# 47-point DFT of later batches as three float32r products, with the inputs taken through a DRAM buffer

## The chip, the core and the metric

The kernel runs on one core of one Trainium2 chip. The time is the device time of one execution in microseconds (us); several executions are timed, and their median is given. The engines are TensorE (PE in the profile, with its weight loads as PEld), VectorE (DVE), ScalarE (ACT), GpSimd (POOL) and SyncE (SP, which here issues nearly all DMAs after the first batch).

## The reference

A convolution along the sequence by a real FFT, and then, for each token, a two-layer network with a rational function between the layers:

```python
X = np.fft.rfft(x, axis=1)                  # x: 8 batches, 3008 positions, 256 channels
y = np.fft.irfft(X * (filt_r + 1j * filt_i), n=3008, axis=1)
h = y.reshape(24064, 256) @ w_in            # 256 x 2048
P = a[0] + a[1] * h + a[2] * h**2 + a[3] * h**3
Q = 1.0 + abs(b[0]) * abs(h) + abs(b[1]) * h**2
out = (P / (Q + 1e-06)) @ w_out             # 2048 x 256
```

## The kernel before

3008 = 64 x 47, so the Fourier transform is split in stages of matrix products. Stage 1 is the 47-point DFT: the input of a batch, laid out beforehand as 96 rows (47 positions and one of padding, times two halves) by 32 x 256 columns (`xp`), is multiplied by a constant 96 x 96 matrix. A batch has eight loads q of 96 x 1024 numbers (tile `xin`, 384 KB each, 4 KB in a row), and each load two products of 96 x 512 (tile `s`, matmul on L298). ACT evicts each product from PSUM into `ev` (`s1e` in the profile), and SP stores the pair into a DRAM buffer `scr1`. Stage 2 loads `scr1` in another layout, multiplies by the 64-point matrix (`y`, L346), by the filter (DVE and POOL), and by the inverse matrix (`z`, L379), and stores into `scr2`. Stage 3 loads `scr2` (tile `tl`), does the inverse 47-point product (`x`, L424), and writes the result as two float32r tiles, `xh` and the remainder `xl`, which feed the network.

Stages 1 to 3 multiply float32 by float32. The network multiplies in float32r: each operand is split into a float32r part and a float32r remainder, and three products hi x hi, lo x hi and hi x lo are summed in PSUM.

The network's work is cut into 752 units: unit i is 512 tokens by 128 of the 2048 hidden columns, 16 units to a token tile. A unit has six float32r products into `h_u` (L457, L458, L460), five activations on ACT, four operations on DVE (L502, `hi_u` on L511, L519, `lo_u` on L525), two on POOL (L497, then L516, the product q * hi), and six float32r products into `o` (L534 to L536). The operations of a unit are spread over several steps: at step i TensorE does the `h_u` products of unit i and the `o` products of unit i-4, and the other engines work on units i to i-3, by a list of lags.

`pipeline` writes this out by hand: for the engines PE, ACT, DVE and POOL the order in the code is the order of execution. At every step at most one piece of the next batch's convolution is put behind the unit's `h_u` products. Pieces are paid from a credit that grows by 0.6 a unit while batch 1 is prepared, and by 0.38 for later batches; the number that a generator yields is a piece's price, and a bare `yield` hands on to the next place in the step, or the next step, without a price. SP's order is not written by hand once the pipeline has begun: a list scheduler puts SP's DMAs where it finds them ready. Every DMA of SP takes one of eight semaphores in turn, and waits for the DMA that had it before.

Batch 0 goes through all stages before the units begin, together with the decoding of the weights' 64-bit words (`bits` and `split`), of which the last four of 16 steps run beside the first units. Batches 1 to 7 are prepared beside the units. The code branches once, on a flag from the scalars, into one of two versions of the pipeline.

Of the kernel before, what the change touches and what calls it, by code (L numbers as in the profile page):

```python
# [9 lines left out]
F32 = mybir.dt.float32  # L10
F32R = mybir.dt.float32r
I32 = mybir.dt.int32
U32 = mybir.dt.uint32
AF = mybir.ActivationFunctionType
ALU = mybir.AluOpType
# [9 lines left out]
NH = 32  # L25
K2 = 24
R1 = 96
C = 256
# [6 lines left out]
XF = 1  # L35
RING = dict(a=4, w=3, q=5, hi=5, lo=4)
GAP = 4
PGAP, XGAP = 1, 1
CPOS = 3
OG = 2  # L40
# [2 lines left out]
EV1, EV2, EVO = "A", "AV", "AV"  # L43
XB, FB = 4, 3
# [12 lines left out]
TT = 512  # L57
# [45 lines left out]
def conv_moe(ctx: ExitStack, tc: tile.TileContext, xp, fr, fi, w_in, w_out, ab, mats, small, sgn, outT):  # L103
    nc = tc.nc
    B = xp.shape[0]

    consts = ctx.enter_context(tc.tile_pool(name="consts", bufs=1))
    dram = ctx.enter_context(tc.tile_pool(name="dram", bufs=3, space=DRAM))
    conv = ctx.enter_context(tc.tile_pool(name="conv", bufs=2))
# [9 lines left out]
    xh = xl = None  # L119
    mats_sb = consts.tile([128, 3, 128], F32, name="mats_sb")  # L120
    small_sb = consts.tile([R1, R1 + GE], F32, name="small_sb")
    a1_sb, e_sb = small_sb[:, :R1], small_sb[:, R1 : R1 + G]
    words = consts.tile([128, 128], F32, name="words_sb")
    sgn_sb, ab_sb, abs_sb, cf_sb = words[:, :K2], words[:, 32:44], words[:, 64:76], words[:, 96:120]
    flag_sb = words[:, 120:121].bitcast(I32)
# [28 lines left out]
    def inverse(y, x, t):  # L154
        v.reciprocal(y, x)
        tt(out=t, in0=x, in1=y, op=ALU.mult)
        ts(out=t, in0=t, scalar1=-1.0, scalar2=2.0, op0=ALU.mult, op1=ALU.add)
        tt(out=y, in0=y, in1=t, op=ALU.mult)

    def square_scalars():  # L160


        x, y, z, p, ip, pq1 = (col(i, 2) for i in (8, 10, 12, 14, 16, 18))
        v.tensor_copy(col(8), A3)
        v.tensor_copy(col(9), B1)
        inverse(y, x, z)

        stt(out=col(14), in0=A2, scalar=0.5, in1=col(10), op0=ALU.mult, op1=ALU.mult)
        stt(out=col(15), in0=B0, scalar=0.5, in1=col(11), op0=ALU.mult, op1=ALU.mult)
        inverse(ip, p, z)  # L170
        v.tensor_copy(IPC, col(16))
        v.tensor_copy(IQC, col(17))
        tt(out=ip, in0=ip, in1=ip, op=ALU.mult)
        tt(out=pq1[:, :1], in0=A1, in1=col(10), op=ALU.mult)
        ts(out=pq1[:, 1:], in0=col(11), scalar1=1.000001, scalar2=None, op0=ALU.mult)
        tt(out=pq1, in0=pq1, in1=ip, op=ALU.mult)
        ts(out=pq1, in0=pq1, scalar1=1.0, scalar2=None, op0=ALU.subtract)
        v.tensor_copy(PK, col(18))
        stt(out=P0, in0=A0, scalar=col(10), in1=col(16), op0=ALU.mult, op1=ALU.mult)
        inverse(IK, col(19), col(12))  # L180
        ts(out=SGN, in0=IK, scalar1=0.0, scalar2=None, op0=ALU.is_ge)
        ts(out=SGN, in0=SGN, scalar1=2.0, scalar2=-1.0, op0=ALU.mult, op1=ALU.add)
        tt(out=AIK, in0=IK, in1=SGN, op=ALU.mult)

        inverse(col(20), col(16), col(12))
        stt(out=col(20), in0=A3, scalar=col(20), in1=AIK, op0=ALU.mult, op1=ALU.mult)
        stt(out=SC, in0=col(11), scalar=col(17), in1=col(20), op0=ALU.mult, op1=ALU.mult)
        for name, c in (("ipc", IPC), ("iqc", IQC), ("ik", IK), ("sc", SC)):
            act_scale[name] = r = nc.scalar.alloc_register(name)
            nc.scalar.reg_load(r, c[:1].bitcast(I32))  # L190
# [4 lines left out]
    class Weights:  # L195
# [14 lines left out]
        def load(self):  # L210
            tag = ("oe", "tl", "oe", "tl", "raw")[self.i % 5] if self.i < HD else ("oe", "xin")[self.i % 2]
            raw = conv.tile([128, 2 * TT], I32, tag=tag, name=f"raw{self.i}", bufs={"xin": XB, "raw": 1}.get(tag))
            self.raw = raw.rearrange("p (n t) -> p n t", t=2)
            (nc.scalar if self.i < HD else nc.sync).dma_start(raw.rearrange("p (a c) -> p a c", a=2), self.src)
# [38 lines left out]
        return wo_sb[:, f // 2, k, c : c + 128]  # L253

    scr1 = [dram.tile([K2, 128, C], F32, tag="scr1", name=f"scr1_{b}") for b in range(B)]
    scr2 = [dram.tile([K2, 128, C], F32, tag="scr2", name=f"scr2_{b}") for b in range(B)]

    def rows(scr):
        return scr.rearrange("k (g m) c -> (k g) m c", m=NH)

    def evac(which, out, in_, i):
        if which[i % len(which)] == "A":
            nc.scalar.activation(out, in_, AF.Copy)
        else:
            nc.vector.tensor_copy(out, in_)
# [17 lines left out]
    def stage1_load(b, q):  # L283
        xin = conv.tile([R1, 2, TT], F32, tag="xin", name=f"xin{b}_{q}", bufs=XB)
        nc.sync.dma_start(
            xin.rearrange("p a b -> p (a b)"), xp[b, :, 4 * q : 4 * q + 4, :].rearrange("p m c -> p (m c)")
        )
        return xin

    def stage1(b, q, xin=None):  # L290

        if xin is None:
            xin = stage1_load(b, q)
        ev = conv.tile([R1, 2, TT], F32, tag="ev", name=f"s1e{b}_{q}")
        for j in range(2):
            yield 0.86
            k, pt = banks.tile(f"s1_{b}_{q}_{j}")
            nc.tensor.matmul(pt[:R1], a1_sb, xin[:, j], start=True, stop=True)  # L298
            yield
            evac(EV1, ev[:, j], pt[:R1], 2 * q + j)  # L300
            banks.done(k, 0.5)
        nc.sync.dma_start(
            rows(scr1[b])[:, 4 * q : 4 * q + 4, :].rearrange("r m c -> r (m c)"), ev.rearrange("p a b -> p (a b)")
        )

    class Stage2:

# [81 lines left out]
    def stage2(b):  # L389
        s = Stage2(b)  # L390
        for q in range(2):
            s.load_filter(q)
            s.load(q)
        for i in range(13):
            if i < 12:
                yield from s.product(i)
            if i > 0:
                yield from s.inverse(i - 1)
            if i % 2 == 0 and i // 2 + 2 < 6:
                s.load_filter(i // 2 + 2)  # L400
                s.load(i // 2 + 2)
            if i > 0 and i % 2 == 0:
                s.store(i // 2 - 1)
# [134 lines left out]
    banks = None  # L538
# [12 lines left out]
    nt = B * S // T  # L551

    def conv_items(b):
        for q in range(8):
            yield from stage1(b, q)
        for _ in range(GAP):
            yield
        yield from stage2(b)

    def run(gen):  # L560
        for _ in gen:
            pass
# [3 lines left out]
    class Decode:  # L566
# [19 lines left out]
        def part(self, k):  # L586
            while self.parted < k:
                weights[self.parted].split()
                self.parted += 1
# [3 lines left out]
    def first_batch():  # L593

        s = Stage2(0)
        s.more = [xpool.tile([128, 6 - FB, 4, C], F32, tag=x, name=f"f{x}") for x in ("xh", "xl")]
        xin = {}
        fl = iter(range(6))

        def do(tokens):  # L600
            for c in tokens:
                if c == "W":
                    dec.load()
                elif c == "D":
                    dec.step()
                elif c == "F":
                    s.load_filter(next(fl))

        nc.scalar.dma_start(ab_sb, ab.rearrange("(o n) -> o n", o=1).broadcast_to([128, 12]))
        nc.scalar.dma_start(small_sb, small)  # L610
        for q in range(XB):
            xin[q] = stage1_load(0, q)
        do("WW")
        nc.scalar.dma_start(mats_sb, mats)
        nc.scalar.dma_start(sgn_sb, sgn)
        load_flag()
        square_scalars()
        for q in range(8):
            run(stage1(0, q, xin.pop(q)))
            if q + XB < 8:  # L620
                xin[q + XB] = stage1_load(0, q + XB)
            do(HA[q])
        for q in range(XB - 1):
            s.load(q)
        for q in range(2):
            s.double_filter(q)
        do(HM)
        for i in range(12 + ZL):
            if i < 12:
                run(s.product(i))  # L630
            if i >= ZL:
                run(s.inverse(i - ZL))
            q, j = divmod(i, 2)
            if j == 0 and q + XB - 1 < 6:
                s.load(q + XB - 1)
            elif j and q + 2 < 6:
                s.double_filter(q + 2)
            if i > ZL and (i - ZL) % 2:
                s.store((i - ZL) // 2)
            do(HB[i])  # L640
        nonlocal xh, xl
        xh, xl = (xpool.tile([128, 2, RX], F32R, tag=x, name=x) for x in ("xh", "xl"))
        for k in range(2):
            run(stage3(k))
        dec.part(HD)
        assert dec.done == dec.loaded == HD
# [99 lines left out]
    with tc.manual_schedule(engines=ENGINES):  # L746
        banks = Banks(8 - T * 2 // TT)
# [70 lines left out]
```

## Time and profile before

| | |
|---|---|
| median of 3 runs | 2541.02 us (2540.35 to 2542.63) |
| profiled execution | 2545.82 us, of which the span of instructions 2543.2 us |
| mean granted TensorE clock | 0.991 |
| stage-1 products | 128, of which 112 for batches 1 to 7 |
| DMA traffic | 208.76 MB, mean 82 GB/s |

In the profile a line begins with the line number in the code, then engine, operation, output and input. Busy time is the time in which an engine had at least one instruction under way. On TensorE matmuls are pipelined, so an instruction's length is more than the distance to the next one, and distances between starts are what counts. The rows of windows give, for a stretch in us, the busy time and the number of instructions of PE, PEld, DVE, ACT and POOL, then the granted clock, the share of the 16 DMA engines' time that was busy, and GB/s. A float32 matmul has two records.

### The profile page before, as it was taken

How to read it: one execution, taken by the hardware profiler on the slowest of the kernel's cores; microseconds unless marked ns; L12 is line 12 of the kernel's file. 1: busy time of each engine (PE TensorE's matmuls, PEld its weight loads, DVE VectorE, ACT ScalarE, POOL GpSimd, SP SyncE). 2: the span in 40 equal slices, each digit the busy share in tenths (PEclk: the TensorE clock that was granted, in tenths of full speed). 3: DMA queues.
4: the chain of work that ended last, by engine and by line, in shares of the span. 5: the costliest groups of instructions: out<-in, count | busy, mean ns of one | idle time of the engine just before them, and what ended most of it. 6: DMA issues, size and time to landing. Idle time of an engine off the chain costs nothing.

```text
span 2543.2 us, 35887 instructions
## 1 busy us (share of the span) xinstructions
PE 2479.4 (97%) x10712; PEld 1934.2 (76%) x10712; DVE 2264.1 (89%) x3549; ACT 2197.0 (86%) x4170; POOL 1850.8 (73%) x1984
## 2 busy tenths in 40 slices
PE   4799999999999999999999999999999999999998
PEld 1467777777777777777777777777777778888887
DVE  4789988999889998899888998899988999999998
ACT  3588889888998889888998889988888889999997
POOL 2468876788668876788667886688767887677676
PEclk7899999999999999999999999999999999999999
DMA  8653341323223332233213332233322210000000
GB/s 239 192 138 114 97 120 48 113 84 98 68 81 93 91 87 64 79 98 96 83 56 106 93 96 70 72 93 99 89 62 89 72 55 28 25 25 17 25 9 19
DMA packets 102813, 208.76 MB, mean 82 GB/s; under 512 B 8752, under 2 KB 58512, under 8 KB 102608
## 3 DMA queue, kind: packets, MB, share of 16 engines
q1 hardware_dynamic: 99568, 199.79, 26.8%
q10 hardware_dynamic: 3040, 6.58, 0.9%
q8 instruction: 87, 1.43, 0.2%
q14 instruction: 118, 0.97, 0.1%
HBM read 131.36 MB, written 74.97 MB: 81 GB/s over the span
## 4 chain that ended last, share of the span: by engine, by line
PE 93%; DVE 2%; DMA 2%; ACT 1%; issue 0%; SPq 0%; ACTq 0%; DVEq 0%
PE o L534 13%; PE o L535 13%; PE o L536 13%; PE h_u L458 13%; PE h_u L457 13%; PE h_u L460 13%; PE x L424 4%; PE s L298 4%; PE y L346 3%; PE z L379 3%; DMA scr<-s1e 1%; DMA fxl<-fi 0%; DVE hi_u L511 0%; DVE h_u L519 0%; ACT q_u L478 0%
## 5 line engine op out<-in xcount | busy, mean ns | idle before, releaser
L516 POOL TENSOR_TENSOR q_u<-q_u,hi_u 128x512 f32<-128x512 f32 x752 | 973.7, 1295 | 493.4 <-DVE hi_u L511 475.7
L534 PE MATMUL o<-hi_u,wo_sb 128*128 128x512 f32 x1504 | 701.0, 466 | 0.0
L465 ACT ACTIVATE q_u<-h_u 128x512 f32<-128x512 f32 x752 | 449.9, 598 | 203.8 <-PE h_u L460 150.8
L511 DVE SCALAR_TENSOR_TENSOR hi_u<-h_u,words_sb,a_u 128x512 fp32r<-128x512 f32 x752 | 561.7, 747 | 60.3 <-ACT a_u L487 57.6
L519 DVE SCALAR_TENSOR_TENSOR h_u<-h_u,words_sb,q_u 128x512 f32<-128x512 f32 x752 | 567.1, 754 | 52.4 <-POOL q_u L516 52.1
L457 PE MATMUL h_u<-xh,wi_sb 128*128 128x512 f32 x1504 | 596.3, 396 | 5.4 <-DVE xl L435 4.0
L535 PE MATMUL o<-lo_u,wo_sb 128*128 128x512 f32 x1504 | 589.6, 392 | 1.6 <-DVE lo_u L525 1.6
L536 PE MATMUL o<-hi_u,wo_sb 128*128 128x512 f32 x1504 | 589.3, 392 | 0.0
L458 PE MATMUL h_u<-xl,wi_sb 128*128 128x512 f32 x1504 | 588.2, 391 | 0.0
L497 POOL TENSOR_SCALAR q_u<-q_u,words_sb 128x512 f32<-128x512 f32 x752 | 579.3, 770 | 3.5 <-ACT a_u L482 3.5
L502 DVE SCALAR_TENSOR_TENSOR h_u<-w_u,words_sb,h_u 128x512 f32<-128x512 f32 x752 | 563.3, 749 | 4.2 <-ACT w_u L472 4.2
L525 DVE TENSOR_TENSOR lo_u<-h_u,a_u 128x512 fp32r<-128x512 f32 x752 | 516.4, 687 | 0.1
L482 ACT ACTIVATE a_u<-q_u 128x512 f32<-128x512 f32 x752 | 475.4, 632 | 0.1
L487 ACT ACTIVATE a_u<-a_u 128x512 f32<-128x512 f32 x752 | 470.4, 626 | 0.0
L478 ACT ACTIVATE q_u<-q_u 128x512 f32<-128x512 f32 x752 | 469.5, 624 | 0.0
L460 PE MATMUL h_u<-xh,wi_sb 128*128 128x512 f32 x1504 | 464.6, 390 | 0.0
L472 ACT ACTIVATE w_u<-h_u 128x512 f32<-128x512 f32 x752 | 443.8, 590 | 0.0
L534 PEld LDWEIGHTS o<-hi_u,wo_sb 128*128 128x128 f32 x1504 | 283.2, 188 | 112.2 <-issue 63.3
L535 PEld LDWEIGHTS o<-lo_u,wo_sb 128*128 128x128 f32 x1504 | 283.2, 188 | 111.3 <-issue 60.0
L457 PEld LDWEIGHTS h_u<-xh,wi_sb 128*128 128x128 f32 x1504 | 283.0, 188 | 73.6 <-DVE lo_u L525 4.3
L458 PEld LDWEIGHTS h_u<-xl,wi_sb 128*128 128x128 f32 x1504 | 283.3, 188 | 64.5 <-issue 4.1
L536 PEld LDWEIGHTS o<-hi_u,wo_sb 128*128 128x128 f32 x1504 | 282.5, 188 | 61.8
(96 smaller groups left out, 1886.7 us busy)
## 6 DMA issues: line engine op xcount, KB each, us to landing
xin<-xp SPq DMA_DIRECT2D x64, 384.0 KB, 3.9
scr<-s1e SPq DMA_DIRECT2D x64, 384.0 KB, 4.1
xin<-scr SPq DMA_DIRECT2D x48, 512.0 KB, 4.9
scr<-ev SPq DMA_DIRECT2D x48, 512.0 KB, 4.7
outT<-oe SPq DMA_DIRECT2D x47, 512.0 KB, 3.3
f<-fr SPq DMA_DIRECT2D x87, 256.0 KB, 4.1
f<-fi SPq DMA_DIRECT2D x87, 256.0 KB, 3.8
tl<-scr SPq DMA_DIRECT2D x44, 480.0 KB, 4.0
```

Source lines behind the costliest of these rows:

```text
L457: nc.tensor.matmul(o, w_in_part(0, f, cc), xh[:, cc, ts], start=cc == 0, stop=False)
L458: nc.tensor.matmul(o, w_in_part(0, f, cc), xl[:, cc, ts], start=False, stop=False)
L460: nc.tensor.matmul(o, w_in_part(1, f, cc), xh[:, cc, ts], start=False, stop=cc == 1)
L497: nc.gpsimd.tensor_scalar(out=self.q, in0=self.q, scalar1=AIK, scalar2=SGN, op0=ALU.mult, op1=ALU.add)
L502: v.scalar_tensor_tensor(out=H, in0=w, scalar=PK, in1=H, op0=ALU.add, op1=ALU.mult)
L511: nc.vector.scalar_tensor_tensor(out=self.hi, in0=self.H, scalar=self.p0, in1=self.a, op0=ALU.add, op1=ALU.mult)
L516: nc.gpsimd.tensor_tensor(out=self.q, in0=self.q, in1=self.hi.bitcast(F32), op=ALU.mult)
L519: nc.vector.scalar_tensor_tensor(out=self.H, in0=self.H, scalar=self.p0, in1=self.q, op0=ALU.add, op1=ALU.subtract)
L525: nc.vector.tensor_tensor(out=self.lo, in0=self.H, in1=self.a, op=ALU.mult)
L534: nc.tensor.matmul(o, w_out_part(0, f, dd), self.hi, start=f == 0, stop=False)
L535: nc.tensor.matmul(o, w_out_part(0, f, dd), self.lo, start=False, stop=False)
L536: nc.tensor.matmul(o, w_out_part(1, f, dd), self.hi, start=False, stop=f == 15)
```

## The change

For batches 1 to 7 stage 1 is done by `stage1_parts` instead of `stage1`. SP first copies each load's 384 KB from `xp` into a DRAM buffer `scr0`, and loads `xin` from there, as a float32r tile. For each half of a load (a "part") ACT copies `xin` into a float32r tile `xh` (one of the tag `raw`, with a single buffer), POOL subtracts it from `xin` in place, and TensorE does three float32r products in place of one float32 product, with the constant matrix split in the same way once at the start (`a1r_sb`). The price of a product goes from 0.86 to 0.69. The part of product i+1 is put between the products and the eviction of product i; before the first product there are three bare yields. The eviction on ACT, the store and the stages behind it stay.

```diff
+    a1r_sb = consts.tile([R1, 2, R1], F32R, name="a1r_sb")
+    scr0 = [None] + [dram.tile([R1, NH, C], F32, tag="scr0", name=f"scr0_{b}", bufs=2) for b in range(1, B)]
+    def stage1_parts(b):
+        xin, his = {}, {}
+        def copy(q):
+            m = slice(4 * q, 4 * q + 4)
+            nc.sync.dma_start(scr0[b][:, m], xp[b, :, m])
+        def load(q):
+            xin[q] = conv.tile([R1, 2, TT], F32R, tag="xin", name=f"xin{b}_{q}", bufs=XB)
+            src = scr0[b][:, 4 * q : 4 * q + 4].rearrange("p m c -> p (m c)")
+            nc.sync.dma_start(xin[q].bitcast(F32).rearrange("p a b -> p (a b)"), src)
+        def part(i):
+            q, j = divmod(i, 2)
+            if j == 0:
+                his[q] = conv.tile([R1, 2, TT], F32R, tag="raw", name=f"xh{b}_{q}", bufs=1)
+            x, hi = xin[q][:, j], his[q][:, j]
+            nc.scalar.activation(hi, x.bitcast(F32), AF.Copy)
+            nc.gpsimd.tensor_tensor(out=x, in0=x.bitcast(F32), in1=hi.bitcast(F32), op=ALU.subtract)
+        for q in range(3):
+            copy(q)
+        load(0)
+        load(1)
+        yield 0.1
+        for _ in range(PART):          # PART = 3
+            yield
+        part(0)
+        for i in range(16):
+            q, j = divmod(i, 2)
+            if j == 0:
+                ev = conv.tile([R1, 2, TT], F32, tag="ev", name=f"s1e{b}_{q}")
+                if q + 3 < 8:
+                    copy(q + 3)
+                if q + 2 < 8:
+                    load(q + 2)
+            yield 0.69
+            k, pt = banks.tile(f"s1_{b}_{q}_{j}")
+            hi, lo = his[q][:, j], xin[q][:, j]
+            nc.tensor.matmul(pt[:R1], a1r_sb[:, 0], hi, start=True, stop=False)
+            nc.tensor.matmul(pt[:R1], a1r_sb[:, 0], lo, start=False, stop=False)
+            nc.tensor.matmul(pt[:R1], a1r_sb[:, 1], hi, start=False, stop=True)
+            yield
+            if i < 15:
+                part(i + 1)
+            evac(EV1, ev[:, j], pt[:R1], i)
...
     def conv_items(b):
-        for q in range(8):
-            yield from stage1(b, q)
+        yield from stage1_parts(b)
...
+        nc.scalar.activation(a1r_sb[:, 0], a1_sb, AF.Copy)
+        nc.gpsimd.tensor_tensor(out=a1r_sb[:, 1], in0=a1_sb, in1=a1r_sb[:, 0].bitcast(F32), op=ALU.subtract)
```

How the queues change. In the lists below a line number is that of the version it is from; the first digit in a name like `xin1_3` is the batch and the second the load, `scr0_4` is the copy buffer of batch 4, `raw15` a piece of the weights, `tl3` a chunk of stage 3, `f11_0` and `f21_0` the filter's two tables for batch 1, and `x5` means that many alike in a row.

SP, from the first entries behind the branch. Before:

```order
L214 DMA raw14_645<-w_out 128x2x512
L418 DMA tl2_668<-scr2_0_88 96x1280
L285 DMA xin1_0_670<-xp 96x1024
L214 DMA raw15_723<-w_out 128x2x512
L285 DMA xin1_1_806<-xp 96x1024
L418 DMA tl3_976<-scr2_0_88 96x1280
L285 DMA xin1_2_889<-xp 96x1024
L418 DMA tl4_1256<-scr2_0_88 96x1280
L285 DMA xin1_3_957<-xp 96x1024
```

SP at the same place, changed (shown without a break up to the fourth load of batch 1):

```order
L320 DMA xin1_1_685<-scr0_1_89 96x1024
L216 DMA raw15_726<-w_out 128x2x512
L315 DMA scr0_2_90<-xp 96x1024 x6
L315 DMA scr0_3_91<-xp 96x1024 x2
L320 DMA xin1_2_759<-scr0_1_89 96x1024
L315 DMA scr0_3_91<-xp 96x1024 x6
L315 DMA scr0_4_92<-xp 96x1024 x8
L315 DMA scr0_5_93<-xp 96x1024
L379 DMA f11_0_1746<-fr 64x1024 x2
L315 DMA scr0_5_93<-xp 96x1024 x5
L474 DMA tl4_1304<-scr2_0_96 96x1280
L379 DMA f21_0_1747<-fi 64x1024
```

The copies of batches 2 to 5 stand ahead of batch 1's fourth load `xin1_3`, which is the next row; ten copies and `tl3` stand ahead of these rows, and the rest of the 56 copies stand between `xin1_3` and the seventh load, `xin1_6`, so that none is left behind that. Between `tl2` and `xin1_6` there are 56 copies, six loads of batch 1, two stores of its products, `tl3` to `tl5`, `raw15` and twelve filter halves of 256 KB.

ACT, in two steps of batch 1 with a product (`a_u` and `q_u` are tiles of units, `s1_1_2_0` and `s1_1_2_1` are the products of load 2). Before:

```order
L465 ACTIVATE q_u7_920<-h_u7_901 128x512
L263 ACTIVATE s1e1_2_891<-s1_1_2_0_908 96x512
L487 ACTIVATE a_u6_883<-a_u6_883 128x512
L478 ACTIVATE q_u7_920<-q_u7_920 128x512
L472 ACTIVATE w_u7_921<-h_u7_901 128x512
L482 ACTIVATE a_u7_919<-q_u7_920 128x512
L465 ACTIVATE q_u8_952<-h_u8_933 128x512
L263 ACTIVATE s1e1_2_891<-s1_1_2_1_940 96x512
```

ACT in the step of product `s1_1_2_1`, changed:

```order
L538 ACTIVATE a_u12_1125<-q_u12_1126 128x512
L521 ACTIVATE q_u13_1162<-h_u13_1141 128x512
L328 ACTIVATE xh1_3_1165<-xin1_3_940 96x512
L266 ACTIVATE s1e1_2_1018<-s1_1_2_1_1148 96x512
L543 ACTIVATE a_u12_1125<-a_u12_1125 128x512
L534 ACTIVATE q_u13_1162<-q_u13_1162 128x512
```

The new Copy (L328), which needs the load `xin1_3`, stands ahead of the eviction and of the unit's further activations. The product also moved from unit 8 to unit 13.

POOL there, changed (before, the rows L553 and L572, then L497 and L516, simply alternated):

```order
L553 TENSOR_SCALAR q_u11_1091<-q_u11_1091,words_sb_80 128x512
L329 TENSOR_TENSOR xin1_3_940<-xin1_3_940,xh1_3_1165 96x512
L572 TENSOR_TENSOR q_u11_1091<-q_u11_1091,hi_u11_1158 128x512
L553 TENSOR_SCALAR q_u12_1126<-q_u12_1126,words_sb_80 128x512
L329 TENSOR_TENSOR xin1_3_940<-xin1_3_940,xh1_3_1165 96x512
```

The subtraction (L329) now stands ahead of the multiplication with `hi_u`. On TensorE one row of L298 becomes three, L350 to L352, at the same place in its step, behind the unit's `h_u` products.

More of the change, by code (lines that the diff above doesn't have):

```diff
@@ L37 @@
 GAP = 4
+PART = 3
 PGAP, XGAP = 1, 1
@@ L304, in stage1 @@
         )
+    def stage1_parts(b):
[40 more added lines that the diff above has]
+            evac(EV1, ev[:, j], pt[:R1], i)
+            banks.done(k, 0.5)
+            if j:
+                m = slice(4 * q, 4 * q + 4)
+                nc.sync.dma_start(rows(scr1[b])[:, m, :].rearrange("r m c -> r (m c)"), ev.rearrange("p a b -> p (a b)"))
     class Stage2:
```

## The prediction

> **What bounds the kernel now.** I read the busy shares and the chain first, then the windows by stage, then who waits for whom.
>
> ```profile
> PE 2479.4 (97%) x10712; PEld 1934.2 (76%) x10712; DVE 2264.1 (89%) x3549; ACT 2197.0 (86%) x4170; POOL 1850.8 (73%) x1984
> DMA  8653341323223332233213332233322210000000
> PE 93%; DVE 2%; DMA 2%; ACT 1%; issue 0%; SPq 0%; ACTq 0%; DVEq 0%
> ```
> ```profile
> 600.00:800.00 200.00, 200.00 (x884) 157.33 (x883) 175.06 (x271) 178.05 (x339) 138.62 (x146) 1.00 0.30 88
> 2300.00:2400.00 100.00, 100.00 (x464) 83.54 (x463) 94.33 (x149) 95.51 (x184) 71.92 (x71) 1.00 0.07 21
> ```
> ```profile
> ACT q_u L465 <- PE h_u L460: 150.8, 316, 2.4
> DVE h_u L519 <- POOL q_u L516: 52.1, 113, 1.0
> ```
> TensorE carries 93% of the chain and is never idle in the two windows, at full clock, with or without stage-1 work beside the units. ACT waits for it (150.8 us before L465). So time taken off TensorE comes off the whole, while nothing else runs out. The DMA row shows spare capacity on average, but 8, 6 and 5 tenths in the first three slices: the start is where transfers are dense.
>
> **What a stage-1 product costs TensorE, and what three would.** TensorE in time around one product of batch 2; columns are start, length, engine, line.
>
> ```profile
> 628.84 0.62 PE L460 MATMUL h_u<-xh,wi_sb 128*128 128x512 f32 x2
> 629.29 1.02 PE L298 MATMUL s<-xin,small_sb 96*96 96x512 f32 x2
> ...
> 632.45 0.62 PE L460 MATMUL h_u<-xh,wi_sb 128*128 128x512 f32 x2
> ...
> 635.16 0.62 PE L460 MATMUL h_u<-xh,wi_sb 128*128 128x512 f32 x2
> ...
> 637.88 0.62 PE L460 MATMUL h_u<-xh,wi_sb 128*128 128x512 f32 x2
> ```
> A unit with the product takes 632.45 - 628.84 = 3.61 us, one without 637.88 - 635.16 = 2.72: the float32 product costs 0.89. The unit's 12 float32r products of the same 512 columns take 2.72/12 = 0.227 each, so three take 0.68, and the gain is 0.21 us. A 96-row float32r product isn't in the trace. It moves as many columns and loads fewer weights than the 128-row one, so I take its 0.227. Bounds: 0.24 (the gain falls to 0.17), and no switch cost at all, which is 0.21.
>
> For batches 2 to 7 that is 96 x 0.21 = 20.2 us. In batch 1 a product stands in nearly every unit (rate 0.6 a unit, against 0.38 later), and there ACT comes into it. ACT in a step that it goes through without idling:
>
> ```profile
> 112.58 0.63 ACT L482 ACTIVATE a_u<-q_u 128x512 f32<-128x512 f32 x1
> ...
> 113.59 0.58 ACT L263 ACTIVATE s1e<-s 96x512 f32<-96x512 f32 x1
> 114.07 0.62 ACT L487 ACTIVATE a_u<-a_u 128x512 f32<-128x512 f32 x1
> ...
> 115.58 0.66 ACT L232 ACTIVATE df<-raw 128x512 f32<-128x512 f32 x1
> ...
> 126.40 0.64 ACT L244 ACTIVATE wi_sb<-df 128x512 fp32r<-128x512 f32 x1
> 126.92 0.64 ACT L482 ACTIVATE a_u<-q_u 128x512 f32<-128x512 f32 x1
> ```
> A unit's five activations and one eviction take 115.58 - 112.58 = 3.00 us, of which the eviction 0.48, so 2.52 without. The added Copy into float32r is priced by L244, also a Copy into float32r: 126.92 - 126.40 = 0.52. A step with a product then takes ACT 3.52, TensorE 2.72 + 0.68 = 3.40. In batch 1 a step goes from 3.60 (the rows below) to 3.52: 16 x 0.08 = 1.3 us. Later there is a product every 0.69/0.38 = 1.82 units: TensorE 1.82 x 2.72 + 0.68 = 5.63, ACT 1.82 x 2.52 + 0.48 + 0.52 = 5.59. TensorE stays ahead, barely; the other stages' steps, longer on TensorE, give ACT room. Gain in all: 20.2 + 1.3 = 21.5 us.
>
> **POOL.** The subtraction, which stands ahead of the unit's multiplication (L516) in POOL's order, has that row's kind, and takes 1.3 us.
>
> ```profile
> L516 POOL TENSOR_TENSOR q_u<-q_u,hi_u 128x512 f32<-128x512 f32 x752 | 973.7, 1295 | 493.4 <-DVE hi_u L511 475.7
> L497 POOL TENSOR_SCALAR q_u<-q_u,words_sb 128x512 f32<-128x512 f32 x752 | 579.3, 770 | 3.5 <-ACT a_u L482 3.5
> ```
> With 1.3 + 0.77 + 1.3 = 3.37 us in a step of 3.40 POOL just holds, and its 475.7 us of waiting for hi_u cover it on average. When it comes late, L519 waits (52.1 us now), then lo_u and L535. Lags of up to four units stand between, so I charge 2 us, with bounds of 0 and 0.12 x 96 = 11.5 us (every later step at ACT's 3.52).
>
> **The copies and SP's queue.** The 56 copies are DRAM to DRAM, 384 KB each, and the queue holds them all ahead of batch 1's last loads, right behind the branch (which was at 105.6). Every entry waits for the one eight transfers back, so SP goes at the pace of the transfers. The trace has no DRAM-to-DRAM transfer. The nearest are the load and the store of the same 96 rows of 4 KB (windows; last two columns are the share of the 16 DMA engines and GB/s):
>
> ```profile
> xin<-xp SPq DMA_DIRECT2D x64, 384.0 KB, 3.9
> ```
> ```profile
> 8.00:12.00 4.00, 4.00 (x6) 1.42 (x5) 3.38 (x26) 0.00 (x0) 0.00 (x0) 1.00 1.02 288
> 25.00:26.00 1.00, 1.00 (x3) 0.29 (x2) 0.26 (x1) 1.00 (x3) 0.00 (x0) 0.50 1.05 418
> 106.00:108.00 2.00, 2.00 (x5) 1.30 (x5) 0.97 (x3) 1.08 (x4) 0.69 (x1) 0.50 0.89 257
> 108.00:110.00 2.00, 2.00 (x8) 1.54 (x7) 0.00 (x0) 0.48 (x1) 1.86 (x2) 0.72 0.97 275
> 120.00:122.00 2.00, 2.00 (x6) 1.52 (x6) 1.85 (x4) 0.81 (x2) 2.00 (x3) 0.50 0.00 0
> 140.00:150.00 10.00, 10.00 (x41) 7.17 (x39) 9.14 (x16) 7.57 (x15) 9.36 (x9) 1.00 1.02 256
> 418.60:423.50 4.90, 4.90 (x23) 4.03 (x22) 4.15 (x7) 4.73 (x10) 2.74 (x4) 1.00 0.28 82
> 564.60:570.00 5.40, 5.40 (x23) 4.09 (x23) 4.82 (x9) 5.40 (x11) 3.49 (x6) 1.00 0.26 97
> ```
> At 8 to 12 us loads alone fill the engines at 288 GB/s: 393 kB in 1.37 us. The lone store at 418.6 takes 0.28 x 4.9 = 1.37 us of all engines. If reading and writing overlap, a copy takes 1.37, and that I take, since both rows have its shape. Lower end: the output's store (512 KB, 564.6) takes 0.26 x 5.4 = 1.40, that is 1.05 for 384 KB, near the best window (418 GB/s, 0.94). Upper end: load and store one after the other, 2.74.
>
> Supply. Up to the load of xin1_6 (products 12 and 13) the queue holds, from 106 us on, 56 copies (76.7 us), seven loads, two stores, three tl loads and one raw load (5.54 MB at 288 GB/s: 19.2 us) and twelve filter halves (3.15 MB at the 256 GB/s of 140 to 150 us: 12.3 us), 108.2 us in all. The rows at 106 and 108 show the engines at 0.89 and 0.97 with what was issued before; that costs some 3 us. A load lands 3.9 us after issue, 2.5 beyond its 1.4 of transfer. So xin1_6 lands at 106 + 3 + 108.2 + 2.5 = 219.7 us.
>
> Demand. ACT's copy for product 12 stands in unit 21 (from 0).
>
> ```profile
> 139.41 0.50 PE L535 MATMUL o<-lo_u,wo_sb 128*128 128x512 f32 x1 [1.23 <-DVE lo_u L525]
> ...
> 140.68 0.39 PE L457 MATMUL h_u<-xh,wi_sb 128*128 128x512 f32 x1
> ...
> 145.65 1.02 PE L298 MATMUL s<-xin,small_sb 96*96 96x512 f32 x2
> ...
> 149.25 1.02 PE L298 MATMUL s<-xin,small_sb 96*96 96x512 f32 x2
> ...
> 152.86 1.25 PE L424 MATMUL x<-small_sb,tl 96*128 96x94 f32 x10
> ...
> 156.74 1.25 PE L424 MATMUL x<-small_sb,tl 96*128 96x94 f32 x10
> ```
> Up to 140 DVE, busy with the weights' decoding, sets the pace (139.41), and its list isn't changed, so unit 7 stays at 140.7. From there the changed order has ten steps with a product (3.52) and four with stage 3 (156.74 - 152.86 = 3.88): 50.7 us, so unit 21 starts at 191.4, and ACT reaches the copy 2.1 later, at 193.5. It would wait 26.2 us. The same sum gives 13 us for xin1_3, 18 for xin1_4 and 24 for xin1_5, so the wait builds up load by load. ACT is in order: behind the Copy stand the unit's activations, then DVE's hi_u and lo_u, then TensorE. TensorE can run on for about 2 us, by the lag of four units, so it loses 24. It comes back with its clock down: 0.50 at 120 to 122, after the idling there. For a few such gaps I add 2 us. Afterwards the queue holds no copies, and later loads are early, as now.
>
> Sum: -21.5 + 24.2 + 2 + 2 = +6.7 us. On the profiled execution (2545.82, 4.80 above the median of 2541.02) that gives 2552.5; on the median, 2548. Bounds: copies at 1.05 shorten the supply by 18, and with no charge for POOL and the clock the sum is -15 (2526); at 2.74 it is +83 (2624).
>
> **The rivals.** *Fast copies, or a covered wait (faster).* At 1.2 us or less a copy, xin1_6 lands by 210, the wait is under 17, and the sum is below -3; at 1.05 it is -11: 2530. For it: the windows with 418 GB/s and with 512 KB in 1.40 us, and that a copy touches no partitions. Against it: the transfers in 4 KB rows run at 256 to 288. It decides at a copy of 1.25 us, where the sum is zero.
> *Slow copies (slower by far).* If reading and writing share what limits them, a copy lies between 1.37 and 2.74; at 1.8 the supply grows by 24 us: 2572. The trace mixes both directions without falling under 256 GB/s, so I give it less. The Trainium skill, "DMA: Bandwidth & Descriptors", section "Latency and other measured facts", gives 214 GB/s per direction for copies between HBM tensors at their full rate: an estimate from it is 393/214 = 1.84 us a copy, by which the sum would be +33 (2574) instead of +6.7. No run here shows it yet.
> *ACT and POOL bound all of stage 1.* Then later steps go at 3.52, the charge of 2 becomes 11.5, and with the wait the time is 2557. ACT's 5.59 against 5.63 speaks for it, its 150.8 us of idling against.
>
> **How the numbers follow.** A copy near the rows' pace (1.2 to 1.6 us), break-even or a little slower: 0.49. Fast or covered: 0.28. Slow: 0.18. ACT and POOL: 0.05. What this kernel can tell from no change is 0.2%, 5 us. The first splits into 0.04 faster (should my demand be early by some us), 0.21 same, 0.24 slower; the second into 0.25 faster and 0.03 same; the others are slower. So 0.29 faster, 0.24 same, 0.47 slower. The forecast is 2548 us. The range, 2523 to 2580, takes in the fast end and slow copies up to 1.9 us; the likeliest case alone covers 2538 to 2561.
>
> **What would show it.** In the changed profile: DMA share near 1 from 106 to about 220 us; ACT waiting for xin<-scr, some 25 us in four or five pieces before 225; TensorE idle there and its clock down; later windows full, L350 to L352 at 0.227 us spacing. No such wait would make the forecast wrong towards 2523; a wait over 50 us, or TensorE idle in stage 1 after 400 us, towards the slow side.

## The result and the profile after

| | before | changed | ratio, 95% interval |
|---|---|---|---|
| median of 6 runs each | 2542.39 us | 2561.03 us (2559.67 to 2563.87) | 1.0072 [1.0062, 1.0082] |
| span of the profiled execution | 2543.2 us | 2558.0 us | |

The change makes the kernel 18.6 us slower. First the page of the changed kernel: busy shares, DMA row, and shares of the chain.

```profile
PE 2467.7 (96%) x10824; PEld 1951.1 (76%) x10824; DVE 2261.3 (88%) x3549; ACT 2231.3 (87%) x4283; POOL 1991.9 (78%) x2097
DMA  8893243232323232322233323322222110000000
PE 86%; DMA 4%; DVE 2%; ACT 2%; POOL 2%; issue 2%; SPq 0%; ACTq 0%; DVEq 0%; POOLq 0%
```

TensorE's busy time fell by 11.7 us while the span grew by 14.8, so TensorE now stands idle for some 26 us more. In the chain its share went from 93% to 86%, and DMA, DVE, ACT and POOL share the rest. In the DMA row the third slice went from 5 to 9 tenths: the copies. Where the idle time lies shows in the windows (start and end; length; busy time and instructions of PE, PEld, DVE, ACT, POOL; clock, DMA share, GB/s). First before, then the changed kernel, from 110 to 220 us:

```profile
110.00:220.00 110.00, 99.76 (x423) 74.60 (x422) 91.37 (x142) 96.21 (x183) 69.41 (x69) 0.98 0.48 133
```
```profile
110.00:220.00 110.00, 75.06 (x327) 58.18 (x328) 70.42 (x110) 74.93 (x149) 68.15 (x62) 0.88 0.86 287
600.00:800.00 200.00, 199.33 (x902) 160.21 (x901) 176.67 (x275) 183.21 (x356) 162.73 (x167) 1.00 0.29 85
2300.00:2400.00 100.00, 100.00 (x462) 83.50 (x461) 94.59 (x150) 95.44 (x184) 72.28 (x71) 1.00 0.07 21
```

In this one stretch TensorE does 24.7 us less (99.76 - 75.06). Later windows are nearly full, but not quite: 199.33 of 200 where before had 200.00. Inside the stretch, slices of 10 us:

```profile
120.00:130.00 10.00, 7.85 (x41) 5.69 (x39) 9.61 (x15) 8.17 (x17) 9.60 (x9) 0.96 1.02 371
160.00:170.00 10.00, 0.00 (x0) 0.00 (x0) 0.00 (x0) 0.00 (x0) 0.14 (x1) 0.59 1.02 301
170.00:180.00 10.00, 5.01 (x14) 3.88 (x15) 3.42 (x5) 5.66 (x12) 1.95 (x2) 0.56 1.03 366
180.00:190.00 10.00, 4.58 (x20) 3.32 (x19) 2.20 (x4) 2.94 (x6) 4.65 (x5) 0.96 1.02 355
```

From 160 to 170 us four engines do nothing at all, POOL one instruction, and the DMA engines are full. What they wait for is in the waits from 100 to 260 us (engine and line, what it waits for: us in total, times, longest):

```profile
ACT s1e L266 <- DMA scr<-s1e: 24.6, 2, 17.6
PE s L350 <- ACT s1e L266: 22.2, 3, 16.0
ACT xh L328 <- DMA xin<-scr: 3.1, 1, 3.1
```

ACT waits 24.6 us on L266, the eviction of a stage-1 product, and only 3.1 us on L328, the Copy that needs a load. The eviction writes `ev` (`s1e`), which has two buffers. The third pair of products needs the buffer of the first pair, and that comes free when the first pair's *store* has landed. In time, SP's queue first, then ACT (start, length, the idle time before it in brackets):

```profile
100.90 3.10 SPq L315 DMA_DIRECT2D scr<-xp  x5
...
113.67 8.88 SPq L315 DMA_DIRECT2D scr<-xp  x8
...
124.49 17.20 SPq L315 DMA_DIRECT2D scr<-xp  x15
...
166.71 0.42 SPq L360 DMA_DIRECT2D scr<-s1e  x1
...
188.65 0.31 SPq L320 DMA_DIRECT2D xin<-scr  x1
```
```profile
174.34 0.59 ACT L266 ACTIVATE s1e<-s 96x512 f32<-96x512 f32 x1 [17.57 <-DMA scr<-s1e]
...
188.67 0.59 ACT L266 ACTIVATE s1e<-s 96x512 f32<-96x512 f32 x1 [7.04 <-DMA scr<-s1e]
```

ACT is ready for the third pair's first eviction at 174.34 - 17.57 = 156.8 us. The first pair's two evictions were at 134.83 and 138.84, but its store is only issued at 166.71, behind copies and filter loads, and lands 7.6 us later. The second wait, 7.04 us, is the same for the fourth pair. So the transfers that the stall hangs on first are batch 1's results on their way out, not its inputs on their way in.

### The profile page after: what moved, and what is told of

Read it like the earlier page. It is cut to its first block, busy times and chain, and to the rows that moved or that the text cites. A ratio compares the mean times of both kernels' runs of the same rounds, so it can differ in the third digit from the quotient of the medians.

```text
span 2558.0 us, 36457 instructions
## 1 busy us (share of the span) xinstructions
PE 2467.7 (96%) x10824; PEld 1951.1 (76%) x10824; DVE 2261.3 (88%) x3549; ACT 2231.3 (87%) x4283; POOL 1991.9 (78%) x2097
## 4 chain that ended last, share of the span: by engine, by line
PE 86%; DMA 4%; DVE 2%; ACT 2%; POOL 2%; issue 2%; SPq 0%; ACTq 0%; DVEq 0%; POOLq 0%
PE o L590 12%; PE o L592 12%; PE o L591 12%; PE h_u L513 12%; PE h_u L514 12%; PE h_u L516 12%; PE x L480 4%; PE y L402 3%; PE z L435 3%; DMA scr<-xp 2%; PE s L351 1%; PE s L352 1%; PE s L350 1%; POOL q_u L572 1%; DMA scr<-s1e 1%
## 5 line engine op out<-in xcount | busy, mean ns | idle before, releaser
L572 POOL TENSOR_TENSOR q_u<-q_u,hi_u 128x512 f32<-128x512 f32 x752 | 974.5, 1296 | 290.3 <-DVE hi_u L567 269.0
L575 DVE SCALAR_TENSOR_TENSOR h_u<-h_u,words_sb,q_u 128x512 f32<-128x512 f32 x752 | 568.2, 756 | 123.3 <-POOL q_u L572 123.0
L590 PE MATMUL o<-hi_u,wo_sb 128*128 128x512 f32 x1504 | 658.5, 438 | 0.0
L592 PE MATMUL o<-hi_u,wo_sb 128*128 128x512 f32 x1504 | 589.4, 392 | 0.0
L553 POOL TENSOR_SCALAR q_u<-q_u,words_sb 128x512 f32<-128x512 f32 x752 | 579.3, 770 | 3.6 <-ACT a_u L538 3.6
L516 PE MATMUL h_u<-xh,wi_sb 128*128 128x512 f32 x1504 | 464.7, 390 | 0.0
```

Source lines behind the costliest of these rows:

```text
L516: nc.tensor.matmul(o, w_in_part(1, f, cc), xh[:, cc, ts], start=False, stop=cc == 1)
L553: nc.gpsimd.tensor_scalar(out=self.q, in0=self.q, scalar1=AIK, scalar2=SGN, op0=ALU.mult, op1=ALU.add)
L572: nc.gpsimd.tensor_tensor(out=self.q, in0=self.q, in1=self.hi.bitcast(F32), op=ALU.mult)
L575: nc.vector.scalar_tensor_tensor(out=self.H, in0=self.H, scalar=self.p0, in1=self.q, op0=ALU.add, op1=ALU.subtract)
L590: nc.tensor.matmul(o, w_out_part(0, f, dd), self.hi, start=f == 0, stop=False)
L592: nc.tensor.matmul(o, w_out_part(1, f, dd), self.hi, start=False, stop=f == 15)
```

## Experiments

Every time is a median beside runs of the kernel before on the same chip; "off" and "on" are differences to those. Kernels that move code have other line numbers.

**One buffer for the copies.** The copies of all batches go through one DRAM buffer, so most of them must wait for the batch before, and 8 to 11 instead of 56 stand ahead of batch 1's stage 1. (In the changed kernel the trace shows no such wait, though the code says `bufs=2`: all 56 copies are issued by 186.2 us, ahead of batch 1's last two loads.)

```diff
-scr0 = [None] + [dram.tile([R1, NH, C], ..., name=f"scr0_{b}", bufs=2) for b in range(1, B)]
+scr0 = [dram.tile([R1, NH, C], F32, tag="scr0", name="scr0_0")] * B
```

> One DRAM buffer for the copies of all batches instead of one per batch: a copy for batch b+1 can be issued only when the load of the same part for batch b is done, so of the 56 copies only 8 to 11 stand ahead of batch 1's loads and stores; everything else as changed. Theory A (the loss is the wait of batch 1 behind the copies on SP's queue; the trace shows 24.7 us more TensorE idle between 100 and 260 us than before): the time falls by about 20 to 25 us, to 2536 to 2541, and the wait of ACT's eviction for a store shrinks from 24.6 us to under 5. Theory B (the loss is ACT's and POOL's added work in batches 2 to 7): it stays above 2553.

Measured: 2533.83 us beside 2543.18, ratio 0.9967 [0.9954, 0.9979], 9.4 off. That is 28.0 us less than the changed kernel (18.6 on), with the same 56 copies elsewhere in the queue, and some 2 us below the range of theory A. The window and the wait of this kernel:

```profile
110.00:220.00 110.00, 100.05 (x442) 79.81 (x443) 93.29 (x145) 100.49 (x198) 90.87 (x86) 0.94 0.58 169
```
```profile
ACT xh L328 <- DMA xin<-scr: 1.9, 1, 1.9
```

TensorE's 100.05 us are what it had before (99.76), and between 100 and 260 us ACT waits for no store. The stall is the copies' place in SP's queue.

**No copies.** The inputs are loaded straight into float32 tiles, ACT and POOL write the high and low part into a float32r tile of their own.

```diff
-xin[q] = conv.tile([R1, 2, TT], F32R, ...)   # loaded from scr0
+xin[q] = conv.tile([R1, 2, TT], F32, ...)    # loaded from xp
-his[q] = conv.tile(..., tag="raw", ...); x, hi = xin[q][:, j], his[q][:, j]; lo = x
+his[i] = conv.tile(..., tag="raw", ...); x, hi, lo = xin[q][:, j], his[i][:, 0], his[i][:, 1]
```

> No copies at all: float32 loads straight from the input, ACT's Copy and POOL's subtraction write the two halves of one float32r tile (single buffer, so that a part's Copy waits for the product before it). Theory A: within 4 us of e1_held, 2532 to 2540; the gain of three float32r products shows, less what ACT and POOL cost. Theory B: above 2553, as the split stays. If copies cost beyond their place in the queue (DMA traffic in all batches), this one is clearly under e1_held.

Measured: 2535.38 us, ratio 0.9969 [0.9956, 0.9981], 7.8 off: not to be told from the kernel with one buffer. Out of batch 1's way the copies cost nothing measurable.

**Batch 1's stores on another queue.** The changed kernel, with batch 1's eight stage-1 stores issued by POOL.

```diff
-nc.sync.dma_start(rows(scr1[b])[:, m, :]..., ev...)
+(nc.gpsimd if b == 1 else nc.sync).dma_start(rows(scr1[b])[:, m, :]..., ev...)
```

> The changed kernel with all its copies, but the eight stores of batch 1's stage-1 pairs are issued by POOL on its own queue. Theory A1 (what is late is the store of the first pairs, issued at 166.7 us behind the copies, which holds the two eviction buffers; 17.6 and 7.0 us of ACT waiting): the time falls by 14 to 20 us, to 2541 to 2547. Theory A2, as the prediction had it (what is late is the loads of batch 1's parts): no change beyond 5 us, at least 2556.

Measured: 2551.80 us, ratio 1.0032 [1.0021, 1.0043], 8.6 on, so 10.0 less than the changed kernel. That lies between the two theories: neither the stores alone nor the loads alone are what is late. ACT's waits from 100 to 260 us:

```profile
ACT xh L328 <- DMA xin<-scr: 16.7, 4, 7.1
```

The wait for the stores is gone, and what was late behind it shows: the loads, 16.7 us in four pieces. Two kinds of transfers are stuck in the same queue; the stores only stop ACT first.

**The copies alone.** The kernel before, with float32 products, but with its inputs taken through the copies.

```diff
+if b:
+    nc.sync.dma_start(scr0[b][:, m], xp[b, :, m])
-nc.sync.dma_start(xin..., xp[b, :, 4 * q : 4 * q + 4, :]...)
+nc.sync.dma_start(xin..., (scr0 if b else xp)[b][:, m]...)
```

> The kernel before with its float32 products, and only the copies through the DRAM buffer added (56, one buffer per batch, put early by the scheduler as in the changed kernel). Theory A: the copies alone cost 20 to 30 us, 2562 to 2572, with TensorE idle between 110 and 200 us. Theory B: within 5 us of before, 2537 to 2547.

Measured: 2585.35 us, ratio 1.0164 [1.0147, 1.0181], 42.2 on, well above the 20 to 30 that theory A gave. From its SP queue, and TensorE's and ACT's waits from 100 to 260 us:

```profile
112.77 39.97 SPq L288 DMA_DIRECT2D scr<-xp  x34
154.05 0.31 SPq L289 DMA_DIRECT2D xin<-scr  x1
```
```profile
PE s L300 <- DMA xin<-scr: 25.2, 2, 13.3
```
```profile
ACT s1e L264 <- DMA scr<-s1e: 29.6, 2, 21.4
```

Here 34 copies stand in one piece ahead of the third load, and loads and stores are both late. Once the queue is through, nothing more is lost: the unit at a quarter of the way starts 39.3 us after its fellow in the profile of before, the last unit 39.5.

So far the stall is settled: it is worth about 28 us, and it is only at the start. But without it the kernel gains 8 to 9 us where the products alone were forecast to gain 21.5. The other six runs ask where that went.

The trace of the one-buffer kernel shows it in steps that are short. After each token tile's last output the code leaves one step without `o` products. It is 1.36 us of `h_u` on TensorE and not 2.72. If stage-1 products fall into this step and its neighbour, TensorE reads:

```profile
1191.30 0.40 PE L350 MATMUL s<-xh,a1r_sb 96*96 96x512 f32 x1
...
1192.91 0.61 PE L516 MATMUL h_u<-xh,wi_sb 128*128 128x512 f32 x2
1193.80 0.47 PE L350 MATMUL s<-xh,a1r_sb 96*96 96x512 f32 x1 [0.28 <-ACT s1e L266]
1194.68 0.47 PE L351 MATMUL s<-xin,a1r_sb 96*96 96x512 f32 x1 [0.41 <-POOL xin L329]
```

The second product starts 2.5 us after the first and waits twice, for the eviction and then for POOL's subtraction. Measured between starts of `o` products over the whole trace, such a pair of steps takes 6.64 to 6.79 us where 4.08 + 2 x 0.71 = 5.50 would do. There are six after 200 us; a seventh, at 181 us, took 6.35.

**No piece in the short step.** The one-buffer kernel, whose pipeline gives no piece of the convolution to the step after a tile's last output.

```diff
-elif credit > 0 and i < n and not active and ...:
+elif credit > 0 and i < n and not active and ... and i != freed + 1:
```

> Edit on the kernel with one buffer for the copies: no piece of the convolution is issued in the step after a tile's last output (the step that holds no output products). Theory A (short steps): where two products of stage 1 stand in such a step and its neighbour, the pair of steps takes 6.65 to 6.81 us instead of 4.08 + 2 x 0.71 = 5.50, seven times in the held kernel's trace, and nine pairs with a stage-2 and a transposing product take 6.13 instead of 5.85: together about 7 x 1.2 + 9 x 0.28 = 11 us, of which the trace shows 5.6 as idle TensorE. Then 2533.8 - 6 to 11 = 2523 to 2528, and TensorE's idle time between 200 and 2000 us falls from 5.6 to under 1. Theory B (the gain is small because the three products cost more than forecast): the same as the held kernel, 2532 to 2536.

Measured: 2527.12 us beside 2542.26, ratio 0.9942 [0.9928, 0.9955], 15.1 off, as theory A gives.

**No split.** The one-buffer kernel with the pieces where they were, without the Copy and the subtraction.

```diff
-part(0)        # and part(i + 1) in each step
-hi, lo = his[q][:, j], xin[q][:, j]
+hi = lo = xin[q][:, j]
```

> Held kernel without the split of the inputs: ScalarE's Copy and GpSimd's subtraction of each part are left out, and the three products all read the loaded tile, so that the low part is not subtracted; the products and transfers are the same in number and shape. Theory A (the split's work on ScalarE and GpSimd holds up the paired steps): 2533.8 - 7 to 10 = 2524 to 2527, no idle TensorE at the products. Theory B (the loss is in what TensorE takes for the three products, 0.71 where 0.68 was forecast): no change but in batch 1, 2531 to 2534.

Measured: 2526.41 us, ratio 0.9938 [0.9923, 0.9953], 15.9 off. This kernel leaves the low part out and serves for the time alone. The pairs of steps now take 5.49 us (those after 200 us). Windows of the one-buffer kernel, of the rule on short steps, and of this one:

```profile
200.00:2000.00 1800.00, 1794.41 (x7920) 1421.11 (x7919) 1623.05 (x2521) 1608.87 (x3101) 1498.12 (x1601) 1.00 0.33 98
```
```profile
200.00:2000.00 1800.00, 1798.04 (x7952) 1428.01 (x7951) 1628.48 (x2532) 1611.07 (x3114) 1500.74 (x1610) 1.00 0.33 98
```
```profile
200.00:2000.00 1800.00, 1799.23 (x7955) 1428.52 (x7954) 1631.65 (x2532) 1584.26 (x3017) 1377.97 (x1511) 1.00 0.33 98
```

TensorE's idle time goes from 5.6 to 2.0 and 0.8 us. With the split's work kept out of the short steps, or taken away, some 6 us come back in either case (5.7 and 6.5): the split costs time in the short steps and nearly nothing elsewhere. POOL's row says the same. DVE's wait for POOL on L575 rose from 52.1 us before to 123.0 in the changed kernel, and in the kernel with the rule it is

```profile
DVE h_u L575 <- POOL q_u L572: 123.4, 198, 1.6
```

so this wait stayed and cost nothing that shows.

**Price put back.** The one-buffer kernel, with 0.86 instead of 0.69 as the price of a product, which leaves four such pairs instead of seven, three of them after 200 us.

```diff
-yield 0.69
+yield 0.86
```

> Held kernel with the pacing price of a stage-1 product put back from 0.69 to 0.86, so that its products lie further apart; four instead of seven paired steps with two such products, three instead of nine with a stage-2 and a transposing product. Theory A: 3 x 1.2 + 6 x 0.28 = 5 us off, 2528 to 2531. Theory B: the same as the held kernel, 2532 to 2536.

Measured: 2531.09 us, ratio 0.9953 [0.9939, 0.9966], 11.2 off, at the upper edge of what theory A gave. The interval overlaps that of the one-buffer kernel, so the times alone do not tell the two theories apart; the three pairs after 200 us still take 6.64 to 6.81.

**Before, profiled again.**

> The kernel before, profiled once more. In the first profile the stage of batch 0 ended about 5 us later than in each of the five changed kernels (load of the last weight tiles at 101.2 us against 95.8 to 96.5). If that is a draw of the run, the second profile shows 95 to 97 us there and a span of 2538 to 2540; if the change brings it, 101 us again and 2543.

Measured: a span of 2543.3 us, in an execution of 2545.92. The load of the weight tiles came at 97.1 us, so its 101.2 in the first profile was a draw, but the first `o` product did not come earlier:

```profile
127.62 0.80 PE L534 MATMUL o<-hi_u,wo_sb 128*128 128x512 f32 x1
```
```profile
128.00 1.42 PE L534 MATMUL o<-hi_u,wo_sb 128*128 128x512 f32 x1
```
```profile
121.82 0.47 PE L590 MATMUL o<-hi_u,wo_sb 128*128 128x512 f32 x1
```

The first two are the profiles of before, the third the changed kernel. Neither expectation held whole: the lead of 6 us at this place comes with the change, but not from where I had named.

**The rule without the split.** The kernel before with `i != freed + 1`.

> Control for the short steps: the kernel before with the rule of the gap kernel (no piece of the convolution in the step after a tile's last output). It has no split, and its own pairs of steps with two products take 5.85 to 5.89 us, which is 4.08 + 2 x 0.89, without idle TensorE. Theory A (the rule helps only since the split makes ScalarE and GpSimd late in short steps): no change, 2540 to 2545. Rival (the rule is an improvement of its own, whatever stage 1 is made of): about 6 us less, 2535 to 2537.

Measured: 2543.40 us beside 2543.71, ratio 0.9998 [0.9989, 1.0007]. The rule is no gain of its own; it removes a cost that the split brought.

**No copies, and the rule.**

> The kernel without copies (loads straight from the inputs, high and low part written by ScalarE and GpSimd to a tile of their own) with the rule of the gap kernel. If copies behind one buffer cost nothing any more, the same as the gap kernel, 2526 to 2529; if their 22 MB still hold something up, 2 to 4 us less, 2523 to 2525.

Measured: 2526.87 us beside 2543.71, ratio 0.9938 [0.9924, 0.9951], 16.8 off, the same as with copies behind one buffer. These two are the fastest full versions here; both beat before and the changed kernel.

## Why the prediction was right or wrong

The forecast of 2548 us, slower by 6.7, had the sign. The measured 18.6 can be split in the same terms, with other sizes (they add up by construction, since each is the difference of two kernels in a row):

| term | forecast, us | measured, us | from |
|---|---|---|---|
| products | -21.5 | -15.9 | kernel without split |
| POOL and ACT | +2 | +6.5 | one buffer (9.4 off) against no split (15.9 off) |
| wait at the start, with the clock | +26.2 | +28.0 | changed (18.6 on) against one buffer (9.4 off) |
| sum | +6.7 | +18.6 | |

Since the medians are differences across several sets of runs, each measured term is good to some 4 to 5 us, by the intervals.

*The products.* The price of three float32r products was too low. TensorE around one product of the changed kernel:

```profile
654.36 0.62 PE L516 MATMUL h_u<-xh,wi_sb 128*128 128x512 f32 x2
654.82 0.40 PE L350 MATMUL s<-xh,a1r_sb 96*96 96x512 f32 x1
655.05 0.39 PE L351 MATMUL s<-xin,a1r_sb 96*96 96x512 f32 x1
655.28 0.39 PE L352 MATMUL s<-xh,a1r_sb 96*96 96x512 f32 x1
655.51 0.40 PE L590 MATMUL o<-hi_u,wo_sb 128*128 128x512 f32 x1
...
657.79 0.62 PE L516 MATMUL h_u<-xh,wi_sb 128*128 128x512 f32 x2
```

The spacing is 0.23, near the 0.227 taken from the 128-row products, but the step takes 657.79 - 654.36 = 3.43, so the three cost 0.71 and not 0.68. For the old product the one step that I had read stands for all: measured from `h_u` to `h_u` like here, the median over the 79 such steps after 200 us is 3.61, or 0.89. So the gain is 0.18 us a product and not 0.21, just above the lower end of 0.17, and 96 x 0.18 = 17.3 us for batches 2 to 7. That agrees with the kernel without the split, whose interval reaches from 11.9 to 19.6 off. An error of 0.03 us in 0.68 took a seventh of the gain, since the gain is a small difference between large numbers.

*POOL and ACT.* The charge of 2 us was inside its bounds (0 to 11.5), and the row on which I saw trouble, L519's wait, grew as feared but without cost. What failed is the average: a product every 1.82 units leaves 5.63 us of TensorE's time for 5.59 of ACT's, but the products do not come evenly, and a short step gives them 1.36 + 0.71. I counted on lags of up to four units; a product has no such lag, its part is split one piece ahead. So the step that failed here is the cover by lags. Whether ACT or POOL alone would be late in the short steps was not tried; the trace shows waits for both.

*The copies.* I took 1.37 us each. The 15 in a row took 17.20 us to issue, at the pace of the transfers: 1.15 each; the 8 before them 1.11, the 34 of the copies-alone kernel 1.18. That is under the 1.25 us at which the rival of fast copies was to decide for "faster". By its rule (56 copies, 0.10 us under that point) the time would have been near 2535, and it was not, for the reason that follows under the wait. The load of xin1_6 was issued at 188.65 us, some 27 us ahead of the time at which I had it (219.7 less 3.9). The copies are 56 x 0.22 = 12 us of that, the queue's start at 100.9 instead of 106 is 5, and the remaining 10 lie in the other transfers, which the record does not split further. In the changed kernel ACT waited 3.1 us for loads in all. The Trainium skill, "DMA: Bandwidth & Descriptors", section "Latency and other measured facts", gives 214 GB/s per direction, for copies of another layout; 1.84 us a copy was the estimate from it. Here 393 kB in 1.15 us are 342 GB/s, and the measurement decides: the rival of slow copies is out.

*The wait.* The mechanism was right: SP's queue, filled with later batches' copies ahead of batch 1's transfers, an in-order ACT behind it, TensorE idle. The size was right within 2 us. But the step that gives it, that what ends the wait is the load of xin1_6, was wrong. I summed the queue's supply of loads only and left batch 1's stores out of the sum, though each holds one of two `ev` buffers. The stores wait in the same queue, and ACT needs the first pair's buffer back at 156.8 us, for an eviction that stands in its order ahead of the Copy that needs xin1_3. With copies at 1.15 us instead of 1.37 my own sum gives a wait of 26.2 - 12 = 14 us. The loads alone, in the kernel with the stores on POOL's queue, cost 8.6 + 9.4 = 18 us, and the stores in SP's queue add 10.0. That the size came out right is luck: copies priced 12 us too long in all stood in for 10 us of stores left out.

*What would show it.* DMA share near 1 from 106: it lasted to 190, not 220. TensorE idle there and the clock down: yes, 0.56 to 0.59 from 160 to 180. ACT waiting for `xin<-scr` some 25 us in four or five pieces: no, 24.6 us for `scr<-s1e` in two; only with the stores on POOL's queue does ACT wait for the loads, 16.7 us in four pieces. Later windows full: nearly; the idle time in stage 1 after 400 us, named as a sign of the slow side, is the short steps. The rival by which ACT and POOL bound all of stage 1 falls: a step with a product goes at 3.43, not 3.52, save in the short ones.

## What to carry to other kernels

When transfers of later work are put into a queue that also carries the present work, list everything of the present work that passes through it, results on the way out and the buffers that they hold as well as inputs, and ask which is needed first. Work that keeps up on average must also keep up in the shortest step that it can land in; where one step is short by construction, keep the piece out of it. A gain that is a small difference of two step times takes over the whole error of each: a price taken from products of another shape, 0.03 us too low for the three, took a seventh of it here.

## What had not been expected of the hardware

With the DMA engines full in both cases (a share of 1.02), copies from DRAM to DRAM ran faster than loads: 342 GB/s (393 kB in 1.15 us) against the 288 GB/s of the loads at 8 to 12 us in the kernel before. In the prediction I had taken both for the same.

The units start earlier in the changed kernel, its first `o` product at 121.82 us against 127.62 and 128.00: in the code the first stage-1 product now stands three hand-ons later, behind the first units' `h_u`. That this order is the cause was not tried, and much of the lead is work put off. Up to the first `h_u` of the fifth unit the kernel before has done one stage-1 product and twenty of the matmuls of L424 more. At the 41st unit all of batch 1's stage-1 products are done in both; the kernel with one buffer is then 5.7 us ahead, but two pieces of some 0.9 us (one each of L346 and L379) behind, so 3.9 us net, of which 16 x 0.18 = 2.9 would be the cheaper products.
